# A fused attention-and-mixer kernel: each quad's first steps move one half slot against its last ones

## The chip, the cores and the metric

The kernel runs on one core of one Trainium2 chip. The core has five engines: PE (TensorE, the matrix unit, with its weight loads PEld), VectorE (DVE), ScalarE (ACT), GpSimd (POOL) and SyncE (SP, which here issues nearly all DMAs). The metric is the device time of one execution in microseconds; a kernel's time is the median over runs. The profile comes from one further execution that the hardware profiler recorded.

## What is computed

Inputs are q, k, v of shape (8 batches, 8 heads, 576 tokens, 64) and phi (8, 8, 576, 32), all fp32. Cut to what matters:

```python
a    = softmax(phi, axis=tokens_to_slots)          # (b, h, s, 32), softmax over the 32 slots
k_m  = a^T k ;  v_m = a^T v                         # per head: 32 x 64
attn = softmax(q k_m^T / 8, axis=slots)             # (b, h, s, 32)
x    = (attn v_m) with heads side by side           # (8, 576, 512)
u    = x + transpose(relu(x^T w_tok1) w_tok2)       # token mixing, 576 -> 256 -> 576
out  = u + relu(u w_ch1) w_ch2                      # channel mixing, 512 -> 1536 -> 512
```

## The kernel before, in words

**Precision.** The large products are made from fp32 numbers split into a high and a low part (`split`, L117), each product from three matmuls: high x high, high x low, low x high. The high part is made by ScalarE, the low part mostly by VectorE.

**Channel mixing is the main stream.** The 8 x 576 rows of u are cut into 9 *chunks* of 512 rows. For each chunk there are NF = 12 slices of the hidden layer. `ch1` (L140) makes one slice with 12 matmuls of 512 columns into a PSUM tile `cp` (two buffers); `high` and `low` (L157, L171) turn it into `hh` (ScalarE) and `hl` (VectorE); `ch2` (L174), 12 matmuls again, adds the previous slice into the four banks `acc0` to `acc3`. At the end of a chunk, `add` (L204) reads the four banks out on VectorE, `turn` (L208) transposes and `store` (L214) sends the rows off.

**The loop and its half slots.** The loop over g = 12 .. 107 (L1386) is the order of the program on every engine, written by hand. Turn g issues:

```python
high, low = chunks[c].ch1(f)      # cp group on PE
run(2 * g - 1, 1)                 # events of odd half slot, k = 1
high(); low()                     # hh on ScalarE, hl on VectorE
run(2 * g, 0)                     # events of even half slot, k = 0
before[0].ch2(before[1])          # acc group on PE (of the previous slice)
run(2 * g, 1)                     # events of even half slot, k = 1
run(2 * g + 1, -1, 0)             # events of odd half slot, k = -1 and k = 0
```

So k = 0 of an even half slot stands between the `cp` and the `acc` group, k = 0 of an odd one between the `acc` group and the next `cp` group, and k = 1 is later still, on the side of the other engines. Everything else is hung into this order with `at(h, fn, k=...)` (L1339). Within one half slot and one k, events run in the order in which they were entered (quads by batch, then the chunks' own). The engines run in this order each for itself; what one needs of another it waits for. An engine with little to do, such as SP, runs ahead of the written order as far as buffers allow.

**Quads.** Attention and token mixing of one batch are made in two *quads* of four heads. Batches 0 and 1 are made ahead of the loop, together with the weights' decoding, by a planner that isn't touched. Batches 2 to 7 (12 quads) are hung into the loop. A quad's steps, with the tiles they write:

- `load_phi`, `load_kv`, `load_q` (DMA by SP), then `phi_max`, `phi_exp`, `phi_sum` (VectorE, GpSimd, ScalarE): softmax of phi;
- `step_kv` (L350, PE tile `kvp`, 40 small matmuls) and behind it `spread_kv` (VectorE and ScalarE: `ms`, `T`, `vb`, `vh`, `vl`); `q_turn` (VectorE: `qT`);
- `step_T` (L416, PE tile `Tp`, one transposition) and a ScalarE copy `kb`;
- `step_s` (L426, PE tiles `sp0`, `sp1`, the scores, eight matmuls each, of 64 x 32 operands) and behind it `sm1` (VectorE: two transpositions to `S`, maximum, subtraction; ScalarE: exp);
- `sm2` (L488): VectorE makes row sums and the product; `spread_nat` (L496) sends S to a DRAM tile `rows` (four DMAs) and reads it back with tokens on partitions as `raw` (two DMAs); then VectorE transposes to `aT`, ScalarE and GpSimd make `ah`, `al`;
- `nat` (L518): `raw` split into `nat` on ScalarE and VectorE ("rows of tokens are taken up");
- `step_A` (L523, PE tile `Ap`, 14 matmuls with w_tok1, from `nat`), `step_R` (L543, PE tile `Rp`), and four `step_u` (L562, PE tiles `u00`, `u01`, `u10`, `u11`, nine matmuls each); behind each u, ScalarE and VectorE read it out (`uh` and `ul` for the rows of its own chunk, `rest` for those of the next).

All the quads' PSUM tiles come from one pool, `pat`, of two banks (tag `at`, L114). A step takes the next bank once the last reader of its earlier tile is done. Single SBUF buffers matter too: `q` and `raw` share one (tag `qT`), `qT` and `nat` share one (tag `big`).

**Where the quads lie.** r is a quad's start: 24 b - 27 for the first and 24 b - 15 for the second of batch b, so two quads are always 12 half slots apart (the first of batch 2 starts at 24, the loop's beginning, and is followed after 9 half slots). Its steps lie at r (kv, with `q_turn` at k = 1), r + 1 (T), r + 2 (scores), r + 3 with k = 1 (`sm2`), r + 7 with k = 1 (`nat`), r + 9 (A), r + 10 (R), r + 11 to r + 14 (u). The second half of one quad therefore overlaps the beginning of the next. The chunks' own events stand at fixed half slots: with h the half slot at which a chunk ends, `add` at h + 1 with k = -1 (ahead of anything at k = 0), `turn` at h + 3 and h + 5, `store` at h + 6, `take` (splitting `rest` for the chunk after next) at h + 7, `residual` on GpSimd at h - 4.

Of the kernel before, what the change touches and what calls it, by code (L numbers as in the profile page):

```python
# [28 lines left out]
def kernel(  # L29
# [34 lines left out]
    NF = FF // P  # L64
# [171 lines left out]
    def mixer(c):  # L236
        if c not in chunks:
            chunks[c] = Chunk(c)
        return chunks[c]
# [1053 lines left out]
    for Q, h0 in ((0, 3), (1, 11)):  # L1293
        qd = quads[1, Q]
# [44 lines left out]
    def at(h, fn, *x, k=0):  # L1339
        events.setdefault((max(h, 0), k), []).append((fn, x))  # L1340

    for b in range(2, B):
        for Q in range(2):
            qd = second if b == 2 and not Q else Quad(b, Q)
            r = 2 * NF * b - (15 if Q else 27)
            if b == 2 and not Q:
                r = 2 * NF
            else:
                at(max(r - 11, 2 * NF), qd.load_phi)
                at(r - 7, qd.phi_max, k=1)  # L1350
                at(r - 4, qd.phi_exp, k=1)
                at(r - 3, qd.phi_sum, k=1)
                at(max(r - 11, 2 * NF), qd.load_kv, k=1)
                at(r - 4, qd.load_q, k=1)
            at(r, qd.q_turn, k=1)
            at(r, qd.step_kv)
            at(r + 1, qd.step_T)
            at(r + 2, qd.step_s)
            at(r + 3, qd.sm2, k=1)
            at(r + 7, qd.nat, k=1)  # L1360
            at(r + 9, qd.step_A)
            at(r + 10, qd.step_R)
            for x in range(4):
                at(r + 11 + x, qd.step_u, x // 2, x % 2)
        at(2 * NF * (b - 1) + 7, lambda b=b: mixer(b).take(), k=1)
    for c in range(CHUNKS):
        h = 2 * NF * (c + 1)
# [79 lines left out]
```

## Time and profile before

| | |
|---|---|
| time, three runs | 820.14, 817.47, 820.19 us, median 820.14 |
| the profiled execution | 819.32 us, span 817.5 from first to last instruction |
| granted TensorE clock | 0.990 (mean) |
| PE busy | 785.3 us, 96% |
| PEld busy | 652.0 us, 80% |
| VectorE busy | 421.4 us, 52% |
| ScalarE busy | 223.2 us, 27% |
| GpSimd busy | 137.2 us, 17% |
| the loop's stretch with quads, 193.0 to 674.5 us | PE busy 480.6 of 481.5 us |
| the tail without quads, 674.5 to 791.9 us | PE busy 117.4 of 117.4 us |

PE is busy nearly all of the time; but matmuls are pipelined and overlap, so a small stall shows less in busy time than in the distance from one group's start to the next. Three views are used below. The chain of waits lists pieces in order of time: start, length, engine, tile, line and count; the shares of the chain by engine stand on the profile's page. The waits view says who waited for whom: total us, times, longest. The timeline has start, length, engine, line, operation, the written tile, the read tiles, shapes, the count of merged instructions and, in brackets, the idle time ahead and what ended it. "SPq" rows are DMA issues on SP. A quad's tiles are named as above, with numbers left out.

### The profile page before, as it was taken

How to read it: one execution, taken by the hardware profiler on the slowest of the kernel's cores; microseconds unless marked ns; L12 is line 12 of the kernel's file. 1: busy time of each engine (PE TensorE's matmuls, PEld its weight loads, DVE VectorE, ACT ScalarE, POOL GpSimd, SP SyncE). 2: the span in 40 equal slices, each digit the busy share in tenths (PEclk: the TensorE clock that was granted, in tenths of full speed). 3: DMA queues.
4: the chain of work that ended last, by engine and by line, in shares of the span. 5: the costliest groups of instructions: out<-in, count | busy, mean ns of one | idle time of the engine just before them, and what ended most of it. 6: DMA issues, size and time to landing. Idle time of an engine off the chain costs nothing.

```text
span 817.5 us, 12023 instructions
## 1 busy us (share of the span) xinstructions
PE 785.3 (96%) x4733; PEld 652.0 (80%) x4733; DVE 421.4 (52%) x699; ACT 223.2 (27%) x430; POOL 137.2 (17%) x136
## 2 busy tenths in 40 slices
PE   6698898999999999999999999999999999999997
PEld 4487677877887878787888888888878788888886
DVE  5898977385446543754456444744375313212115
ACT  4565645322222222222213221222123211210110
POOL 2135442300130002100121012101310300202000
PEclk9979999999999999999999999999999999999999
DMA  8999463035331522343323432252314100200202
GB/s 209 234 220 228 117 169 89 1 87 112 77 93 33 117 65 45 75 92 87 61 59 67 116 56 76 51 133 43 88 34 77 29 1 2 52 0 1 52 0 53
DMA packets 171128, 65.41 MB, mean 80 GB/s; under 512 B 112320, under 2 KB 168384, under 8 KB 171072
## 3 DMA queue, kind: packets, MB, share of 16 engines
q1 hardware_dynamic: 169984, 64.13, 35.1%
q8 instruction: 37, 0.61, 0.3%
q10 hardware_dynamic: 1088, 0.52, 0.3%
q14 instruction: 19, 0.16, 0.1%
HBM read 51.64 MB, written 12.98 MB: 79 GB/s over the span
## 4 chain that ended last, share of the span: by engine, by line
PE 87%; DVE 5%; SPq 3%; DMA 3%; issue 1%; ACT 1%; DVEq 0%; ACTq 0%
PE acc L188 34%; PE cp L149 34%; PE u L581 8%; PE Ap L541 3%; DMA rawc<-in_moe_w_ch_dram 2%; PE kvp L355 2%; PE sp L433 1%; PE Rp L560 1%; DVE rawc L643 1%; PE end L188 1%; SPq L926 1%; DVE rawc L658 1%; SPq L274 1%; DMA raww<-in_moe_w_tok_dram 1%; PE kvp L958 1%
## 5 line engine op out<-in xcount | busy, mean ns | idle before, releaser
L188 PE MATMUL acc<-hh,c 128*128 128x512 f32 x832 | 276.8, 394 | 0.0
L188 PEld LDWEIGHTS acc<-hh,c 128*128 128x128 f32 x832 | 157.2, 189 | 32.8 <-DVE o L206 0.5
L125 DVE SCALAR_TENSOR_TENSOR hl<-cp,hh 128x512 fp32r<-128x512 f32 x104 | 71.6, 689 | 203.7 <-ACT hh L122 203.6
L149 PE MATMUL cp<-uh,c1h 128*128 128x512 f32 x432 | 171.5, 397 | 0.0
L149 PE MATMUL cp<-ul,c1h 128*128 128x512 f32 x432 | 168.5, 390 | 0.0
L149 PE MATMUL cp<-uh,c1l 128*128 128x512 f32 x432 | 168.4, 390 | 0.0
L188 PE MATMUL acc<-hl,c 128*128 128x512 f32 x416 | 163.3, 393 | 2.2 <-DVE hl L125 2.2
L122 ACT ACTIVATE hh<-cp 128x512 fp32r<-128x512 f32 x104 | 62.2, 598 | 226.1 <-PE cp L149 226.1
L149 PEld LDWEIGHTS cp<-uh,c1h 128*128 128x128 f32 x432 | 81.1, 188 | 23.8 <-issue 8.2
L149 PEld LDWEIGHTS cp<-uh,c1l 128*128 128x128 f32 x432 | 81.1, 188 | 17.4
L149 PEld LDWEIGHTS cp<-ul,c1h 128*128 128x128 f32 x432 | 81.2, 188 | 15.5
L188 PEld LDWEIGHTS acc<-hl,c 128*128 128x128 f32 x416 | 78.6, 189 | 17.2 <-DVE hl L125 2.5
L200 POOL TENSOR_TENSOR o<-uh,ul 128x512 f32<-128x512 f32 x36 | 46.3, 1315 | 119.8 <-issue 70.7
L479 POOL TENSOR_TENSOR al<-aT,ah 128x576 fp32r<-128x576 f32 x16 | 23.3, 1455 | 255.9 <-issue 176.7
L594 ACT COPY rest<-u 128x288 f32<-128x288 f32 (+8 forms) x48 | 15.3, 320 | 93.0 <-PE u L581 92.0
L581 PE MATMUL u<-w2h,Rh 128*128 128x288 f32 x128 | 38.1, 298 | 0.0
L581 PE MATMUL u<-w2l,Rh 128*128 128x288 f32 x128 | 38.0, 297 | 0.0
L581 PE MATMUL u<-w2h,Rl 128*128 128x288 f32 x128 | 37.9, 296 | 0.0
L308 DVE TENSOR_REDUCE pr<-phi 128x128 f32<-128x640 f32 x27 | 35.1, 1302 | 5.2 <-DMA phi<-in_phi_dram 5.2
L602 DVE TENSOR_TENSOR ul<-u,uh 128x288 fp32r<-128x288 f32 (+8 forms) x48 | 16.8, 355 | 38.7 <-ACT uh L596 38.6
L541 PE MATMUL Ap<-w1h,nat 128*128 128x256 f32 x144 | 29.2, 294 | 1.5 <-DVE nat L1028 1.5
L441 DVE STREAM_TRANSPOSE S<-sp 128x288 f32<-128x288 f32 x32 | 15.0, 478 | 29.9 <-PE sp L433 28.9
(146 smaller groups left out, 968.8 us busy)
## 6 DMA issues: line engine op xcount, KB each, us to landing
out_dram<-rows SPq DMA_DIRECT2D x32, 256.0 KB, 4.8
kv<-in_k_dram SPq DMA_DIRECT2D x15, 512.0 KB, 4.2
kv<-in_v_dram SPq DMA_DIRECT2D x15, 512.0 KB, 5.5
q<-in_q_dram SPq DMA_DIRECT2D x192, 36.0 KB, 2.1
rawc<-in_moe_w_ch_dram SPq DMA_DIRECT2D x48, 128.0 KB, 5.6
rawc<-in_moe_w_ch_dram SPq DMA_DIRECT2D x12, 512.0 KB, 6.7
phi<-in_phi_dram SPq DMA_DIRECT2D x16, 256.0 KB, 4.5
rows<-S SPq DMA_DIRECT2D x48, 72.0 KB, 2.1
```

Of the source, the lines that this page charges most:

```text
L122: nc.scalar.activation(out=h, in_=ps, func=AF.Relu)
L125: nc.vector.scalar_tensor_tensor(out=l, in0=ps, scalar=0.0, in1=f32(h), op0=ALU.max, op1=ALU.subtract)
L149: nc.tensor.matmul(ps, l[:, a, w], r[:, a], start=a == 0 and x == 0, stop=a == NKK - 1 and x == 2,)
L188: nc.tensor.matmul(ps, l_[f // 2][:, f % 2, a * P : (a + 1) * P], r[:, w], start=f == start and x == 0, stop=f == end - 1 and x == 2,)
L200: nc.gpsimd.tensor_tensor(out=s.o[:, a], in0=f32(s.uh[:, a]), in1=f32(s.ul[:, a]), op=ALU.add)
L308: nc.vector.tensor_reduce(out=m.rearrange("p (i m) -> p i m", i=4), in_=s.pt.rearrange("p i j m -> p i m j"), axis=AX.X, op=op,)
L355: nc.tensor.matmul(s.kvp[32 * i : 32 * i + 32, : 2 * D], s.pt[:n, i, j, :], s.kv[i][:n, :, j, :], start=j == 0, stop=j == NC - 1,)
L479: nc.gpsimd.tensor_tensor(out=s.al, in0=s.aT, in1=f32(s.ah), op=ALU.subtract)
L541: nc.tensor.matmul(ps[:, :TT], a, w, start=x == 0, stop=x == len(mm) - 1)
L581: nc.tensor.matmul(ps[:, :HALF], a, r, start=x == 0, stop=x == len(mm) - 1)
L594: nc.scalar.copy(out=rest[0][:, kk, o : o + HALF - n], in_=ps[:, n:HALF])
L602: nc.vector.tensor_tensor(out=ch.ul[:, kk, to], in0=ps[:, :n], in1=f32(ch.uh[:, kk, to]), op=ALU.subtract)
```

## The change

The start of every quad but the very first becomes one half slot later (its r), which moves the loads, the phi steps, kv, T and scores. The distances of A, R and u from r shrink by one, so for these quads they stay at their absolute half slot; in the first quad of batch 2, whose r stays, they come one half slot earlier. `sm2` keeps its distance of 3 but loses its k = 1, and `nat` comes at r + 6 instead of r + 7. As r is now even where it was odd, steps that stood between `acc` and `cp` now stand between `cp` and `acc`, and the other way round; k = 1 events change sides in the same way.

```diff
     for b in range(2, B):
         for Q in range(2):
             qd = second if b == 2 and not Q else Quad(b, Q)
-            r = 2 * NF * b - (15 if Q else 27)
+            r = 2 * NF * b - (14 if Q else 26)
             if b == 2 and not Q:
                 r = 2 * NF
             else:
...
             at(r, qd.step_kv)
             at(r + 1, qd.step_T)
             at(r + 2, qd.step_s)
-            at(r + 3, qd.sm2, k=1)
-            at(r + 7, qd.nat, k=1)
-            at(r + 9, qd.step_A)
-            at(r + 10, qd.step_R)
+            at(r + 3, qd.sm2)
+            at(r + 6, qd.nat, k=1)
+            at(r + 8, qd.step_A)
+            at(r + 9, qd.step_R)
             for x in range(4):
-                at(r + 11 + x, qd.step_u, x // 2, x % 2)
+                at(r + 10 + x, qd.step_u, x // 2, x % 2)
```

## The prediction

> **What bounds the kernel now.** I read the page first (totals and the chain of waits), then the weight loads' waits, then the chain piece by piece around one quad, then VectorE, ScalarE and the DMA queue there.
>
> ```profile
> span 817.5 us, 12023 instructions
> PE 87%; DVE 5%; SPq 3%; DMA 3%; issue 1%; ACT 1%; DVEq 0%; ACTq 0%
> PEld sp L433 <- DVE ul L602: 3.0, 4, 0.9
> PEld sp L433 <- ACT rest L594: 2.8, 7, 0.4
> ```
>
> TensorE (PE) holds 87% of the chain. The others lie mostly ahead of the main loop. So a reordering gains only where it removes a stall of PE, and costs only where it makes one. Among PE's waits one line belongs to the steps that move: the score products (`sp`), in 11 of 12 quads, wait for whoever reads the last bank that `u` wrote (`ul` on VectorE four times, the copy `rest` on ScalarE seven times). The next two blocks are the chain (start, length, what): the first quad of the loop, whose scores stand between a `cp` and an `acc` group, and a later one, whose scores follow a `u` group.
>
> ```profile
> 167.16 0.11 PE Tp L418
> 167.27 2.75 PE cp L149 x12
> 170.02 0.65 PE sp L433 x16
> 170.67 2.96 PE acc L188 x12
> ```
>
> ```profile
> 496.37 1.20 PE u L581 x9
> 497.57 1.36 PE kvp L355 x40
> 498.94 2.95 PE cp L149 x12
> 501.88 1.19 PE u L581 x9
> 503.07 0.11 PE Tp L418
> 503.18 2.79 PE acc L188 x12
> 505.96 1.20 PE u L581 x9
> 507.17 1.18 PE sp L433 x16
> 508.34 2.96 PE cp L149 x12
> 511.31 2.72 PE acc L188 x12
> ...
> 527.62 1.67 PE Ap L541 x14
> ```
>
> The same 16 small matmuls take 0.65 us where both banks are free and 1.18 us right behind `u`: the second eight need the bank that `u11` has just filled, so the two halves no longer overlap. In the first three later quads (batch 3 and the first of batch 4) it is worse; first and last of the three, sp start, then start of the group behind:
>
> ```profile
> 247.85 0.69 PE L433 MATMUL sp<-qT,kb 64*32 64x288 f32 x8
> ...
> 249.38 0.50 PE L149 MATMUL cp<-uh,c1h 128*128 128x512 f32 x1
> ...
> 334.58 0.69 PE L433 MATMUL sp<-qT,kb 64*32 64x288 f32 x8
> ...
> 336.05 0.50 PE L149 MATMUL cp<-uh,c1h 128*128 128x512 f32 x1
> ```
>
> That is 1.53 and 1.47 us.
>
> **The change part by part.** *1. kv, T and scores move one half slot, A, R and u stay.* The start offset grows by one and A, R, u lose one or two, so in absolute half slots A, R and u of every quad but the first stay. Only `step_kv`, `step_T`, `step_s` (with `q_turn`, the phi steps and the loads) come one half slot later against them. Quads of a batch are 12 half slots apart, so kv now shares a half slot with the previous quad's u10, T with u11, and the scores stand alone between a `cp` and an `acc` group, exactly as in the first quad's block. The two `at` banks are used alternately (the second score half waits for u11's bank, the first doesn't). Afterwards the order is u10, kvp, u11, Tp, sp0, sp1; u11's readers have a whole `cp` group of 2.7 us to finish, and Tp's one reader too. PE's work is the same, so I add the ten pieces of the later quad in both orders. Before: 1.20 + 1.36 + 2.95 + 1.19 + 0.11 + 2.79 + 1.20 + 1.18 + 2.96 + 2.72 = 17.66. After, a large group costing 2.95 behind kvp or sp and 2.74 otherwise: 1.20 + 2.74 + 1.19 + 1.36 + 2.95 + 1.20 + 0.11 + 2.74 + 0.65 + 2.96 = 17.10. So the order itself is free (0.03) and the gain is the scores' 1.18 - 0.65 = 0.53. Ten quads get it: seven at 0.53 are 3.71, three at 1.50 - 0.65 = 0.85 are 2.55, together 6.26 us. The second quad of batch 2 doesn't: the first quad's u also move up by one, so its scores still stand behind a u (u10 in place of u00), at the same price. The first quad's own scores wait for nothing already.
>
> *2. What hides the moved side steps.* VectorE's vector chain behind kvp (to `T`, `vb`) and `q_turn` used to end before Tp and sp; kvp to Tp was 2.95 + 1.19 us and stays 2.95 + 1.20, Tp to sp was 2.79 + 1.20 and becomes 2.74. `kb` needs one copy after Tp, and qT has all of the time since kvp: cost nothing, from a cover of 2.7 us. SP runs ahead of the written order: phi and kv loads wait for buffers, the q loads for `nat` (their buffer was `raw`), the stores behind them for the queue. All come later by up to 2 to 3 us with several half slots to spare; nothing on PE.
>
> *3. `sm2` goes from "end of half slot 3" to "start of half slot 3" of a quad that begins one later.* In the instruction streams this is one place down, past whatever stands at k=-1. In the second quad of a batch nothing does. In the first quads of batches 3 to 7 (five) it is the four `add` of the ending chunk. With the scores also one `cp` later, the path scores, softmax, `rows` to DRAM, `raw` back, `nat`, A gets shorter from both sides, since A stays. This is where a stall can arise, so here is the path with its prices: VectorE (S turns to the subtraction, hl, row sums, adds, next hl), ScalarE, then SP's rows out and raw in (the first quad's and the slowest), and at the end the one copy that waited for raw, the landing times of raw over all quads and the weight load that opens A.
>
> ```profile
> 507.85 1.04 DVE L441 STREAM_TRANSPOSE S<-sp 128x288 f32<-128x288 f32 x2 [3.89 <-PE sp L433]
> ...
> 509.71 0.76 DVE L451 TENSOR_TENSOR S<-S,mx 128x576 f32<-128x576 f32 x1
> 512.03 0.69 DVE L125 SCALAR_TENSOR_TENSOR hl<-cp,hh 128x512 fp32r<-128x512 f32 x1 [1.56 <-ACT hh L122]
> 512.64 0.74 DVE L460 TENSOR_REDUCE sm<-S 128x18 f32<-128x576 f32 x1
> ...
> 515.43 2.44 DVE L206 TENSOR_TENSOR o<-acc,o 128x512 f32<-128x512 f32 x4
> 517.79 0.68 DVE L125 SCALAR_TENSOR_TENSOR hl<-cp,hh 128x512 fp32r<-128x512 f32 x1
> ```
>
> ```profile
> 515.53 0.67 ACT L475 CAST ah<-aT 128x576 fp32r<-128x576 f32 x1 [3.54 <-DVE aT L471]
> 516.84 0.60 ACT L122 ACTIVATE hh<-cp 128x512 fp32r<-128x512 f32 x1 [0.63 <-PE cp L149]
> ```
>
> ```profile
> 177.12 1.99 SPq L500 DMA_DIRECT2D rows<-S  x4
> 180.78 0.38 SPq L505 DMA_DIRECT2D raw<-rows  x1
> ...
> 514.72 2.39 SPq L500 DMA_DIRECT2D rows<-S  x4
> 518.78 0.38 SPq L505 DMA_DIRECT2D raw<-rows  x1
> ```
>
> ```profile
> 183.60 0.82 ACT L118 CAST nat<-raw 128x512 fp32r<-128x512 f32 x2 [1.12 <-DMA raw<-rows]
> 184.39 1.05 DVE L119 TENSOR_TENSOR nat<-raw,nat 128x512 fp32r<-128x512 f32 x2
> DMA to landing us min/median/max: 2.5/2.9/3.4
> 527.24 0.19 PEld L541 LDWEIGHTS Ap<-w1h,nat 128*128 128x128 f32 x1
> ```
>
> On the clock of the later quad, with its u at 496.37 as before: the sum above up to T, then `cp`, ends at 509.86. hl follows 0.72 later (512.03 against 511.31), 510.58, and holds VectorE 0.61 (to 512.64): 511.19. S turns to the end of the subtraction are 2.62 (507.85 to 510.47): 513.81; the `acc` group behind the scores has ended by 513.47, so the adds run at once, 2.36 (515.43 to 517.79): 516.2. Row sums to the rows' issue are 2.08 (512.64 to 514.72): 518.3, where it was 514.72. Rows to raw takes 3.66 (177.12 to 180.78), raw to the copy 2.82 (to 183.60), copy to the end of `nat` 1.84 (to 185.44): 526.6. A's first weight load came at 527.24 and now comes 0.53 sooner, 526.7. So in these five quads `nat` is ready 0.1 us before it is needed. In the second quads of the batches the adds' 2.36 drop out, of which the exponential on ScalarE takes back some 0.7 (an estimate from ah's 0.67 for as many elements): 1.7 us remain, no stall. Both ends of the five: none, or, with the slowest rows to raw seen (4.06 in place of 3.66) and the slowest landing (3.4, not 2.82), 0.9 us. I take 0.25 a quad, nearer the end that the ordinary rows give, because a late weight load is also laid bare (0.19): 1.25 us in all.
>
> The hl that sits behind sm2 in the same five quads is my second doubt. From the rows' issue: ah starts 0.81 later (515.53 against 514.72) and takes 0.67, then hh 0.60 and hl 0.68, so 521.1; the `acc` group that reads it starts at 513.47 + 3 x 2.72 = 521.6. It fits by 0.5, at no cost; late by more than that it would stall PE one to one.
>
> **The sum.** -6.26 + 1.25 = -5.0 us against the profiled execution's 819.32 (span 817.5 and 1.8 around it): 814.3. The median of the three runs shown, 820.14, is 0.82 above that execution, so for a median I write 815.1.
>
> **The rivals.**
>
> *The round trip is shorter than I add up.* Only one copy in 12 ever waited for raw, so 2.82 is a single reading; the least landing is 2.5. At 2.5 nat comes 0.3 sooner, no A waits, and only the 6.26 remains: 820.14 - 6.26 = 813.9. The two hops of the rows above take 3.66 - 1.99 + 2.82 = 4.5 us. By the Trainium skill (DMA: Bandwidth & Descriptors, Latency and other measured facts) a DMA has a fixed cost of about 2 us, less when HBM is lightly loaded; two hops would then be 4.0, an estimate from that page, and by it this rival would hold. The rows are longer, and I go by them.
>
> *The round trip eats most of it.* With 0.9 us in each of five quads, 4.5 of the 6.26 go: 818.4. For: the slowest rows above are of this kernel; against: they never came together.
>
> *The scores keep their wait.* If what holds the second eight is not u11's bank (say each large group ahead delays them), the gain is nil, and A, then 0.53 later, waits for nothing either: 820.1. Against: the first quad's block has the very order that all get, at 0.65.
>
> *Slower: A waits for raw in all the quads.* If the round trip becomes w longer than forecast, the five quads wait about w, the five second ones w - 1.7. Slower than 824.2 needs 5w + 5(w - 1.7) = 6.26 + 4.1, so w = 1.9: a landing of 4.7 us. Transfers of 256 KB to the output do take that:
>
> ```profile
> out_dram<-rows SPq DMA_DIRECT2D x32, 256.0 KB, 4.8
> ```
>
> It would need the kv loads or a store to overlap raw; the kv loads now start when kvp ends, some 15 us ahead of the rows, and the stores wait on the queue behind nat. Unlikely.
>
> **How the numbers follow.** About 0.5% (4.1 us) is what a measurement of this kernel can tell from no change: under 816.0 is faster, over 824.2 slower. Forecast (0.1 to 0.5 us in each of the five, 814.4 to 816.4): 0.50, four fifths of it faster. Shorter round trip: 0.20, nearly all faster. Long round trip: 0.16, same. Scores keep their wait: 0.08, same. Slower: 0.06. So faster 0.60, same 0.34, slower 0.06. The range goes from 812.8 (no A waits, and half of the spread of the runs, 817.47 to 820.19, below) to 818.8 (A's 0.9 in five quads and a little noise); it leaves out the last two cases and tails.
>
> **What would show it.** In the changed profile: sp of ten quads 0.65 us between `cp` and `acc`, and no wait of sp for `ul` or `rest` but in one quad; rows issued some 3.6 us later in the first quad of batches 3 to 7 and nat's copy there waiting for raw (DMA); a wait of PE's weight load at Ap for nat of 0 to 0.9 us, five times; none for hl at `acc`. Wrong if sp stays at 1.18, if Ap waits in second quads too, or if a wait appears at Tp or kvp (then the banks rotate otherwise).

## The result, and the profile after

| | before | after |
|---|---|---|
| median (lowest to highest; four runs each) | 819.96 us (817.47 to 820.19) | 811.85 us (811.5 to 811.85) |
| the profiled execution | 819.32 us | 811.5 us |
| start of the loop's first scores, after the first instruction (the *stretch ahead*) | 169.96 us | 168.49 us |
| from there to the first matmul of PE's last tile, `end` (the *loop*) | 632.71 us | 626.34 us |

The ratio is 0.9912 [0.9896, 0.9928]: 8.1 us less, where 5.0 were forecast, and the median lies just below the forecast range (812.8 to 818.8). The last two rows split the two profiles at points of PE that both have. The loop became 6.37 us shorter; another 1.47 came from ahead of it, where both kernels issue the same instructions.

The page of the changed kernel, its totals and its chain of waits:

```profile
span 809.7 us, 12041 instructions
PE 783.0 (97%) x4733; PEld 652.2 (81%) x4733; DVE 419.1 (52%) x699; ACT 223.4 (28%) x430; POOL 142.0 (18%) x136
...
PE 86%; DMA 3%; SPq 3%; DVE 3%; issue 2%; POOL 1%; ACT 1%; DVEq 0%; POOLq 0%
```

PE still holds the chain. Of the weight loads' waits, those of `sp` for the reader of a bank have gone from eleven to one (total us, times, longest):

```profile
PEld sp L433 <- DVE ul L602: 0.9, 1, 0.9
```

The one left is the second quad of batch 2, as forecast. The chain around the quad that the prediction took (its u is at 490.72 here, at 496.37 before), in order of time:

```profile
490.72 1.20 PE u L581 x9
491.92 2.74 PE cp L149 x12
494.67 1.18 PE u L581 x9
495.84 1.36 PE kvp L355 x40
497.21 2.95 PE acc L188 x12
500.16 1.21 PE u L581 x9
501.36 0.11 PE Tp L418
501.47 2.75 PE cp L149 x12
504.22 0.65 PE sp L433 x16
504.86 2.96 PE acc L188 x12
...
515.99 2.72 PE acc L188 x12
518.71 2.72 PE cp L149 x12
521.42 1.67 PE Ap L541 x14
```

These are the forecast's ten pieces: from 490.72 to the end of the `acc` group at 507.82 they take 17.10 us, the figure of the prediction. The scores take 0.65. `Ap` takes 1.67, as before, and among the waits of the weight loads none is of `Ap` for a `nat` of the loop (L118, L119): A waits for nothing.

The path to A in the same quad, on VectorE, on ScalarE, on SP and on the weight loads:

```profile
507.89 2.47 DVE L206 TENSOR_TENSOR o<-acc,o 128x512 f32<-128x512 f32 x4
510.28 0.74 DVE L460 TENSOR_REDUCE sm<-S 128x18 f32<-128x576 f32 x1
...
514.38 0.69 DVE L125 SCALAR_TENSOR_TENSOR hl<-cp,hh 128x512 fp32r<-128x512 f32 x1 [1.24 <-ACT hh L122]
...
519.93 1.01 DVE L119 TENSOR_TENSOR nat<-raw,nat 128x512 fp32r<-128x512 f32 x2 [1.86 <-ACT nat L118]
```

```profile
519.28 0.82 ACT L118 CAST nat<-raw 128x512 fp32r<-128x512 f32 x2 [2.60 <-DMA raw<-rows]
```

```profile
512.35 2.12 SPq L500 DMA_DIRECT2D rows<-S  x4
516.30 0.38 SPq L505 DMA_DIRECT2D raw<-rows  x1
```

```profile
521.04 0.19 PEld L541 LDWEIGHTS Ap<-w1h,nat 128*128 128x128 f32 x1
```

The adds now stand ahead of the row sums. The rows are issued 21.63 us after the quad's u (512.35 - 490.72), forecast 21.93, before 18.35 (514.72 - 496.37). The copy of `raw` waits for the DMA, in this quad and in the eleven others. `nat` ends at 520.94 (519.93 + 1.01), 0.10 us ahead of A's first weight load; in the five first quads of batches 3 to 7 this margin is 0.06 to 0.54 us.

### The profile page after: what moved, and what is told of

Same layout as the page of the kernel before. It is cut to its first block, busy times and chain, and to the rows that moved or that the text cites. A ratio compares the mean times of both kernels' runs of the same rounds, so it can differ in the third digit from the quotient of the medians.

```text
span 809.7 us, 12041 instructions
## 1 busy us (share of the span) xinstructions
PE 783.0 (97%) x4733; PEld 652.2 (81%) x4733; DVE 419.1 (52%) x699; ACT 223.4 (28%) x430; POOL 142.0 (18%) x136
## 4 chain that ended last, share of the span: by engine, by line
PE 86%; DMA 3%; SPq 3%; DVE 3%; issue 2%; POOL 1%; ACT 1%; DVEq 0%; POOLq 0%
PE acc L188 35%; PE cp L149 34%; PE u L581 8%; DMA rawc<-in_moe_w_ch_dram 3%; PE Ap L541 3%; PE kvp L355 2%; PE Rp L560 1%; PE end L188 1%; PE sp L433 1%; SPq L926 1%; POOL c L669 1%; DVE rawc L643 1%; POOL c1l L669 1%; SPq L278 1%; SPq L274 0%
## 5 line engine op out<-in xcount | busy, mean ns | idle before, releaser
L188 PE MATMUL acc<-hh,c 128*128 128x512 f32 x832 | 279.7, 397 | 0.0
L341 POOL PARTITION_ALL_REDUCE psr<-pr x11 | 17.4, 1585 | 79.6 <-PE cp L149 69.7
```

The costliest lines, as they stand in the source:

```text
L188: nc.tensor.matmul(ps, l_[f // 2][:, f % 2, a * P : (a + 1) * P], r[:, w], start=f == start and x == 0, stop=f == end - 1 and x == 2,)
L341: nc.gpsimd.partition_all_reduce(s.r, m, P, RED.add)
```

## The experiments

The first four ran beside the kernel before on one chip (its median there was 818.73 us), the last three on another (818.36). In the table, time and its difference are medians over runs; stretch ahead and loop are those of one profile each, split as above.

| kernel | time, us | less the kernel before | ratio [95%] | stretch ahead | loop | loop less 632.71 |
|---|---|---|---|---|---|---|
| scores_only | 811.87 | -6.9 | 0.9932 [0.9907, 0.9957] | 167.24 | 626.79 | -5.92 |
| scores_ahead | 818.71 | 0.0 | 0.9999 [0.9979, 1.0020] | 169.73 | 632.35 | -0.36 |
| sm2_first | 823.19 | +4.5 | 1.0058 [1.0034, 1.0083] | 172.11 | 636.62 | +3.91 |
| A_early | 822.81 | +4.1 | 1.0069 [1.0041, 1.0097] | 172.55 | 635.64 | +2.93 |
| after_again | 812.16 | -6.2 | 0.9922 [0.9891, 0.9952] | 168.97 | 626.36 | -6.35 |
| before_again | 818.75 (one) | | | 169.38 | 632.70 | -0.01 |
| u_gap | 811.47 | -6.9 | 0.9910 [0.9884, 0.9937] | 169.84 | 625.35 | -7.36 |

The loop repeats to 0.02 us between two profiles of one kernel (632.71 and 632.70, 626.34 and 626.36), so it shows tenths that a median can't.

### scores_only: is it the scores alone?

The kernel before, with nothing moved but the scores and `sm2` (all quads but the first):

```diff
-            at(r + 2, qd.step_s)
-            at(r + 3, qd.sm2, k=1)
+            late = 0 if b == 2 and not Q else 1
+            at(r + 2 + late, qd.step_s)
+            at(r + 3 + late, qd.sm2, k=1 - late)
```

> The kernel before, with only step_s one half slot later (and sm2 with it, at the start of the half slot behind) in all quads but the first of batch 2; kv, T, q_turn, phi, loads and A, R, u stay where they were. Theory 1 (the whole gain of the loop is the scores' wait for the bank that u11 filled): sp takes 0.65 us in ten quads and in the second quad of batch 2 too (its scores then stand behind u01, so perhaps still 1.2 to 1.7 there), and the loop is 6.3 us shorter than before, as in the changed kernel. Theory 2 (part of it comes from kv and T standing elsewhere): less than 5 us. The stretch ahead of the loop, which was 1.47 us shorter in the profile of the changed kernel, is not touched by either: if that was chance, about 813.7 in all; if it goes with the change of kv and loads, also 813.7, and with any change behind it 812.

Measured: 811.87 us, loop -5.92, scores 0.65 us in ten quads. This is near the first theory and well above the 5 us of the second: the scores' new place brings 5.92 of the 6.37 us, and the rest of the change adds 0.45.

### scores_ahead: is it the bank?

The kernel before, with the scores in the same half slot, but issued ahead of the previous quad's last u and not behind it. If small matmuls were slow merely because they stand behind a `u` group, this would bring the full gain; if u11's bank holds them up, the scores take 0.65 us and the wait must turn up elsewhere.

```diff
-            at(r + 2, qd.step_s)
+            at(r + 2, qd.step_s, k=0 if b == 2 and not Q else -1)
```

> The kernel before, with the scores in the same half slot but ahead of the previous quad's u instead of behind it. Theory 1 (it is the bank): sp takes 0.65 us, and u11, which now needs the bank of the first score half, waits for its transposition on VectorE, 0.4 to 0.6 us in place of it; the loop gains 0 to 2.5 us, about 818. Theory 2 (small matmuls behind a u group are slow in themselves): sp 0.65, no wait at u11, the full 6 us, about 814.

Measured: ratio 0.9999, loop -0.36. Its weight loads' waits, and its chain around one quad:

```profile
PEld u L581 <- DVE S L441: 12.2, 11, 1.1
```

```profile
505.01 0.66 PE sp L433 x16
505.67 0.02 issue
505.70 0.49 DVE S L441
506.19 0.04 issue
506.24 1.46 PE u L581 x9
507.69 2.74 PE cp L149 x12
```

The scores do run in 0.66 us. Now u waits for their reader: 11 waits, 12.2 us by the weight loads (in the chain above, PE goes without work from 505.67 to 506.24, 0.57 us). The bank is the cause. Swapping the order passes the wait on; a large group put between the two, as in the changed kernel, hides it.

### sm2_first: was it right to put sm2 behind the adds?

The changed kernel, with `sm2` where it stood in the engines' order before, ahead of the ending chunk's adds. The prediction saw the adds in front of `sm2` as pure cost (2.36 us on the path to A).

```diff
-            at(r + 3, qd.sm2)
+            at(r + 2, qd.sm2, k=1)
```

> The changed kernel with sm2 ahead of the adds again (k=1 of the half slot before). Theory 1 (no A waits in the changed kernel, its nat is ready 0.1 to 0.5 us ahead in the five first quads): rows issue 2.4 us sooner there, nat's copy hardly waits for raw, and the time is the same, within 0.5 us of 811.85. Theory 2 (A or hl at acc loses something there that the profile does not show): up to 1.25 us faster.

Measured: 823.19 us, slower than the kernel before. The loop is 10.28 us longer than the changed kernel's: 2.06 for each of the five quads where a chunk ends. VectorE, PE and the chain there:

```profile
520.60 0.78 DVE L471 STREAM_TRANSPOSE aT<-S 128x576 f32<-128x576 f32 x1
521.31 2.45 DVE L206 TENSOR_TENSOR o<-acc,o 128x512 f32<-128x512 f32 x4
```

```profile
522.10 0.47 PE L188 MATMUL acc<-hh,c 128*128 128x512 f32 x1 [1.77 <-ACT ah L475]
```

```profile
522.10 3.00 PE acc L188 x12
```

The adds read the four `acc` banks of the ended chunk. Behind `sm2` they begin only at 521.31, and the next chunk's first `acc` group, which overwrites `acc0`, begins at 522.10, when the first of the four adds (2.45 / 4 = 0.6 us each) has just ended; PE idles 1.77 us. The row names ScalarE's `ah`, which `acc` doesn't read and which ends at about the same time. That it is the adds follows from what `acc` reads and writes; it wasn't tried separately. Neither theory foresaw this. With the scores half a slot later, `sm2` must go behind the adds; what the prediction charged as a cost is what lets the change pay.

### A_early: how near is A to waiting?

The changed kernel with A one half slot (some 2.7 us) earlier. Theory 1 is the prediction's: the path to A ends with the end of `nat`. Theory 2: `nat` could end later without harm, since A's first matmuls read the high part alone.

```diff
-            at(r + 8, qd.step_A)
+            at(r + 7, qd.step_A)
```

> The changed kernel with A one half slot earlier (behind an acc group, one cp group of 2.72 us sooner), to measure how near the edge nat is. Theory 1 (the margins that the profile shows, 0.06 to 0.54 us in five quads and 1.4 to 2.2 in seven, are real): PE waits at Ap for nat, 2.2 to 2.7 us in the five and 0.6 to 1.4 in the others, 12 + 6 = 18 us in all, about 830. Theory 2 (nat could be later without harm, since A's first matmuls need only the high part): half of that or less, under 821.

Measured: 822.81 us; the loop is 9.30 us longer than the changed kernel's, about half of what theory 1 expects. The weight loads' waits for `nat` add up to the same, 6.2 + 3.2 = 9.4 us:

```profile
PEld Ap L541 <- ACT nat L118: 6.2, 5, 1.7
PEld Ap L541 <- DVE nat L119: 3.2, 8, 0.7
```

One quad on PE, ScalarE and VectorE:

```profile
529.11 0.39 PE L541 MATMUL Ap<-w1h,nat 128*128 128x256 f32 x1 [1.28 <-ACT nat L118]
529.33 0.28 PE L541 MATMUL Ap<-w1l,nat 128*128 128x256 f32 x1
529.83 0.50 PE L541 MATMUL Ap<-w1h,nat 128*128 128x256 f32 x2 [0.22 <-DVE nat L119]
```

```profile
528.44 0.82 ACT L118 CAST nat<-raw 128x512 fp32r<-128x512 f32 x2 [2.64 <-DMA raw<-rows]
```

```profile
529.09 1.01 DVE L119 TENSOR_TENSOR nat<-raw,nat 128x512 fp32r<-128x512 f32 x2 [1.88 <-ACT nat L118]
```

A's first matmul starts 0.67 us after ScalarE's copies start (529.11 - 528.44), long before `nat` is done at 530.10. Its third, which needs the low part, starts 0.74 after VectorE's subtraction starts. Theory 2 holds for the mechanism. Its numbers were just missed: 9.30 us is a little over half of 18, and with the changed kernel's 811.85 it gives 821.15, not less than 821. The remaining 1.7 us of the median of 822.81 are not explained by the loop; the profiled execution (824.84 us) had a stretch ahead of 172.55 us, the longest of nine, but the other five runs have no profile.

### after_again and before_again: where do the other 1.5 us come from?

The two kernels unaltered, on another chip. Theory 1 says that the stretch ahead varies by chance; theory 2, that the change shortens it.

> The changed kernel once more, unaltered, for a second profile and many runs beside the kernel before on one chip. Theory 1 (the loop gains 6.4 us, and the 1.5 us that the first pair of profiles differs by ahead of the loop is chance): first scores of the loop anywhere from 167 to 173 us as in the six profiles so far, loop from there to the closing products 626.3 us again, and a ratio over many runs near 1 - 6.4/819 = 0.9922. Theory 2 (the change also shortens the stretch ahead of the loop): first scores again 1.5 us sooner than in before_again, ratio near 0.990.

> The kernel before, unaltered, for a second profile. Theory 1: the loop from its first scores to the closing products takes 632.7 us again; the stretch ahead of it may differ from 169.96 us by two or three. Theory 2: that stretch is 169.5 to 170.5 again.

Measured: 812.16 us and a ratio of 0.9922, as the loop alone would give (1 - 6.35 / 818.36 = 0.9922). That it agrees to the last digit is luck: the interval [0.9891, 0.9952] holds theory 2's 0.990 as well, so the ratio doesn't decide. The first scores of the loop in the two chains, the kernel before's first:

```profile
169.45 0.65 PE sp L433 x16
```

```profile
169.04 0.65 PE sp L433 x16
```

They are 0.4 us apart now, where it had been 1.47. Over all nine profiles the stretch has the same instructions on every engine and took 167.2 to 172.6 us: 167.24 to 169.96 in the four that are the kernel before or made from it, 168.49 to 172.55 in the five that are the changed kernel or made from it. So nothing speaks for the change shortening the stretch, and theory 1 is borne out.

### u_gap: the one wait that is left

The changed kernel, with the last two u of the loop's first quad half a slot later, so that the next quad's scores no longer stand behind a u:

```diff
-                at(r + 10 + x, qd.step_u, x // 2, x % 2)
+                gap = 1 if b == 2 and not Q and x > 1 else 0
+                at(r + 10 + x + gap, qd.step_u, x // 2, x % 2)
```

> The changed kernel, and in the first quad of batch 2 the last two u one half slot later, so that the second quad's scores stand alone there too. Theory 1 (a wait for the bank of a u just made): the one sp that still took 1.67 us takes 0.65, the loop is 1.0 us shorter than the changed kernel's 626.3, the time 0.1% below its. Theory 2: that sp has another reason (first use of a buffer), and nothing changes.

The chain at these scores, first in after_again, then in u_gap:

```profile
203.68 1.19 PE u L581 x9
204.87 0.02 issue
204.89 0.41 ACT uh L596
205.30 0.02 issue
205.32 0.47 DVE ul L602
205.79 0.04 issue
205.84 0.69 PE sp L433 x8
```

```profile
201.81 2.75 PE cp L149 x12
204.56 0.65 PE sp L433 x16
205.20 2.96 PE acc L188 x12
```

The first block shows the wait with its steps: u writes the bank, ScalarE and VectorE read it one after the other, and only then do the second eight score matmuls start. In u_gap they don't wait, and the loop is 625.35 us, 1.0 shorter than the changed kernel's. It is the best of these kernels by its loop; the medians of 811.47 and 812.16 don't tell it from the changed kernel.

## Why the prediction was right and wrong

**The bank and the gain of the order (step 1): right.** Forecast 6.26 us, measured 6.37 in the loop. From one A to the next the gain is 0.89, 0.81 and 0.82 us in the three quads forecast at 0.85, 0.55 in the seven forecast at 0.53, and 0.02 in the second quad of batch 2. scores_ahead shows the cause, scores_only that the scores' place carries nearly all of it.

**The moved side steps (step 2): right.** `kvp`, `Tp` and the loads make no new wait of PE.

**A's wait (step 3): this is the step that failed.** The prediction charged 0.25 us in each of five quads, 1.25 us; the measured wait is nil in all twelve. The end of the path was right: the end of `nat` was forecast 30.2 us after the quad's u (526.6 - 496.37) and came at 30.22 (520.94 - 490.72); the margin was forecast as 0.1 and is 0.10 us in this quad. That it fits so well is partly luck, since errors of the pieces cancel: the rows were issued 0.30 us sooner than forecast, rows to raw took 3.95 for 3.66, raw to the copy 2.98 for 2.82, the copy to the end of `nat` 1.66 for 1.84. What was wrong is its last event. A needs the copies' start + 0.67 (519.28 + 0.67 = 519.95) for its first matmul at 521.26, and the subtraction's start + 0.74 (520.67) for its third at about 521.5. That leaves 1.3 and 0.8 us, where the prediction saw 0.1 and added a charge for nearness. A_early gives both numbers; the trace of before had no case of an A that waited in the loop, but the order of `nat`'s parts and of A's matmuls stood in the code. The second doubt, `hl` behind `sm2`, fit by 0.9 us (it ends at 514.38 + 0.69 = 515.07, its `acc` group starts at 515.99) against a forecast of 0.5.

**The slower rival, and what it overlooked.** It looked for danger where A waits for `raw`. The danger lay on the other side: had `sm2` stayed ahead of the adds, the next chunk's `acc` would have waited, 10.3 us in sum (sm2_first), and the change would have lost.

**The range.** With A's charge at nothing, the prediction's own sum is 820.14 - 6.26 = 813.9, its first rival's figure, though for another reason: that rival has the round trip shorter, and it wasn't. This is still inside the range. Of the 3.3 us between 815.1 and 811.85, A's charge is 1.25 and the order's larger gain 0.1; the other 1.9 us don't come from the loop. In the two profiles 1.47 of it lies in the stretch ahead, and the larger group of runs on another chip has a difference of 6.2 us and not 8.1; so it was the luck of a few runs. The low end of the range allows half of the spread of three runs for this, 1.4 us (which would make it 812.5; the prediction has 812.8). Both were too narrow: 22 runs of the kernel before on one chip went from 814.09 to 822.0.

**The page's rule and the trace.** By the Trainium skill (DMA: Bandwidth & Descriptors, Latency and other measured facts) two hops at about 2 us would take 4.0, an estimate from that page. The estimate counts the fixed cost alone and no time for moving the bytes. Over the changed kernel's twelve quads, the time from the end of the last issue of the rows to the copy's start is 4.25 to 4.97 us: here 516.30 - 512.35 - 2.12 = 1.83 and 519.28 - 516.30 = 2.98, together 4.81. The measurement decides: the round trip was not the shorter one.

**What stays open.** Why the stretch ahead of the loop takes 167.2 us one time and 172.6 another. In it the same load of weights was issued at 27.22 us in one profile and at 29.05 in another, and the profile's DMA share is 0.90 to 1.08 in its first two stretches of 40 us. In the first 40 us the granted clock was lowest, 0.83 and 0.87, in the two executions with the longest stretch (A_early and sm2_first), and 0.90 to 1.00 in the others without an order to be seen. Whether the loads or the clock come first wasn't tried.

## What to carry to other kernels

When a step waits for a PSUM bank that the step just ahead of it has filled, look for a large group to put between them; swapping the two only hands the wait on. Follow a path to the first part that its reader takes, not to the end of the whole tile, and don't charge for a margin merely because it is small (what 0.1 us would cost, these runs don't show: A had 0.8 us to spare). When a step is moved past others on an in-order engine, ask who waits for those others as well: here the adds had to go first, because the main stream's next group needed their banks.

## What the runs showed of the hardware

Sixteen score matmuls, in two groups of eight, take 0.65 us from the first to the next group's start when both PSUM banks are free, and 1.18 when the second bank is still being read. Eight of them alone have a row of 0.69 (in after_again, above): with free banks the two groups run side by side. The stretch of DMA-heavy work ahead of the loop varied by 5 us between executions with the same instructions, while the loop behind it, 626 to 637 us of PE work, repeated to 0.02 us in both pairs of profiles of one kernel, at a granted clock of 1.00.
